# First stage of an attention and mixer kernel: root and evictions in front of scalings, one scaling on VectorE, token products by x tile

## The chip, the cores and the metric

The kernel runs on one core of a Trainium2 chip. A core has five engines with an instruction queue each: TensorE (PE; its weight loads are listed apart as PEld), VectorE (DVE), ScalarE (ACT), GpSimd (POOL) and SyncE (SP, which here only issues transfers). They work side by side and wait for one another through semaphores. The metric is the device time of one execution in microseconds (us); before the change it is 775.88 us, the median of three runs from 775.59 to 776.39.

## The reference

Two blocks in a row, in float32. Attention without a softmax, for each of 8 batches and 8 heads, with a norm over the head's 64 columns:

```
kv  = einsum('bhsd,bhse->bhde', k, v)          # k, v, q: (8, 8, 576, 64)
out = einsum('bhsd,bhde->bhse', q, kv)
rms = sqrt(mean(out * out, axis=-1) + 1e-06)
x   = out / rms * g_norm                       # then (8, 576, 512), heads side by side
```

A mixer over x: first along the sequence (tokens), then along the columns (channels), each with its residual:

```
h  = relu(xt @ w_tok1) @ w_tok2                # xt: x with its last axes swapped
u  = x + h transposed
out = u + relu(u @ w_ch1) @ w_ch2
```

Here w_tok1 is 576 x 256, w_tok2 256 x 576, w_ch1 512 x 1536 and w_ch2 1536 x 512.

## The kernel before, in words

Batches are worked in pairs, four of them. A sequence of 576 rows is cut into four tiles of 128 rows and a rest of 64; the rests of the two batches of a pair share a ninth tile. So a pair has x tiles 0 to 3 (first batch), 4 to 7 (second batch) and 8 (both rests). In the step names a group `c` is two of these tiles: `c` 0 and 1 belong to the first batch, 2 and 3 to the second, 4 is the rest.

The order of the work is written out by hand, as lists of strings: `start` for the attention of the first pair, `middle` for the second pair's attention between the first pair's token mixing, `steady` for the others; the channel part follows. `play` goes through a list and calls each named step, and all engines get their instructions in just this order. An instruction that waits holds up those behind it on the same engine, and no others. The steps around the change are:

- `kv{s}{h}`: k by v of batch `s` of the pair, one half of the heads: 40 instructions on PE, into a PSUM tile ps_kv. `e{s}{h}` evicts it to SBUF as kvp (line 389 on DVE for the first batch of the first pair, else the helper's line 132 on ACT).
- `a{c}{t}`: q by kvp for one x tile, into one of two PSUM buffers, ps_o (ps_r for the rest). All matmuls are recorded at line 135.
- `q{c}{t}`: the squares of that result (ACT, line 455); `g{c}{t}`: the result times g_norm, to x (DVE, line 451). These two read the PSUM buffer, one after the other, and free it.
- `t{c}{t}`: sums of squares (DVE, line 472); `m{c}`: mean (DVE, line 477); `r{c}`: square root (ACT, line 482); `i{c}`: four small DVE instructions (lines 486 to 491) that give the inverse with a correction step.
- the scaling of an x tile by its inverse: `s{c}{t}` on ACT, eight instructions of 64 columns each (line 505), or `d{c}{t}` on DVE, one instruction (line 509).
- `h{s}{t}`: token product for batch `s` and one half `t` of the 256 token columns: the four x tiles of that batch against w_tok1, added up in a PSUM buffer ps_h. `h0{t}{j}` is the part of x tile `j` alone, and exists for the first batch. A float32 matmul is two PE instructions. `hr` adds the rest tile and applies the relu.
- `w{n}{k}`: steps that fetch and decode one block of the token weights: `k` 0 fetches, 1 is two ACT instructions, 2 to 4 are DVE instructions. Blocks 0 and 1 and the rest block 2 hold w_tok1, blocks 3 and 4 hold w_tok2.
- `j14`: 14 products of the identity with itself on PE (28 instructions, ps_j), whose result nobody reads (`keep_warm`, line 1332).
- `l{s}`, `lq{s}`, `lr{s}`: loads of k and v, of q, and of the rest of q for a batch of the next pair, issued on SP.

k, v and q of the first two batches are issued ahead of the list (lines 1275 to 1283).

Of the kernel before, what the change touches and what calls it, by code (L numbers as in the profile page):

```python
# [20 lines left out]
def kernel(  # L21
# [39 lines left out]
    J, JJ, HF = 4, 5, 64  # L61
    LO = P * J
    assert D == 64 and DM == 512 and S == LO + HF and B % 2 == 0
    NC, NF, NTOK = DM // P, DCH // P, DTOK // P
# [49 lines left out]
    def do(f, *a, **kw):  # L114
        return lambda: f(*a, **kw)
# [6 lines left out]
    def dma(o, i, engine=nc.sync):  # L122
        keep(engine.dma_start(o, i))  # L123

    def tensor_add(o, a, b, op=ALU.add, engine=nc.vector):
        keep(engine.tensor_tensor(out=o, in0=a, in1=b, op=op))  # L126

    def relu(o, a):
        keep(nc.scalar.activation(o, a, AF.Relu))  # L129

    def copy(o, a):
        keep(nc.scalar.copy(o, a))  # L132

    def matmul(*a, **kw):
        keep(nc.tensor.matmul(*a, **kw))  # L135
# [78 lines left out]
    def get_tok1(i):  # L214

        rows = words(moe_w_tok1)[:LO].rearrange("(i j p) n w -> i p j n w", j=2, p=P)
        return block(2 * DTOK, lambda raw: [(raw.rearrange("p (j n) w -> p j n w", j=2), rows[i])], w_tok1[i])

    def get_tok1_rem():
        w = words(moe_w_tok1)[LO:]  # L220
        return block(DTOK, lambda raw: [(raw[:HF], w), (raw[HF:], w)], w_tok1r)
# [37 lines left out]
    def t_sums(b):  # L259

        def step(o, x, y):
            return lambda: tensor_add(b(o), b(x), b(y), ALU.subtract)

        return [step(5, 7, 1), step(6, 3, 5), step(7, 3, 7), step(4, 2, 6)]
# [92 lines left out]
    def x_of(pair, i):  # L357

        return X[pair, i // 2][:, i % 2]
# [176 lines left out]
    def token_mixing(pair, seeds, aside=()):  # L536
        h1, acc = {}, {}

        def tok1(side, t, js=range(J)):
            if js[0] == 0:  # L540
                acc[side, t] = ps["h"].tile([P, DM], F32, name="ps_h", tag="h")
            for j in js:
                matmul(acc[side, t], lhsT=w_tok1[j // 2][:, j % 2, ts(t, P)],
                                 rhs=x_of(pair, side * J + j), start=(j == 0), stop=False)

        def tok1_rem():
            for t in range(NTOK):
                for side in range(2):
                    r = ds(side * HF, HF)
                    matmul(acc[side, t], lhsT=w_tok1r[r, ts(t, P)],  # L550
                                     rhs=x_of(pair, 8)[r], start=False, stop=True)
            for side in range(2):
                h1[side] = hp_.tile([P, NTOK, DM], F32, name="h1", tag="h1")
                for t in range(NTOK):
                    relu(h1[side][:, t], acc[side, t])

        def seed(i):


            acc[i] = ps["h"].tile([P, DM], F32, name="ps_u", tag="h")  # L560
            copy(acc[i], x_of(pair, i))

        def tok2(i):
            if i not in seeds:
                n = "o" if i in aside else "h"
                acc[i] = ps[n].tile([P, DM], F32, name="ps_u", tag=n)
            first = i not in seeds
            if i < 8:
                for t in range(NTOK):
                    matmul(acc[i], lhsT=w_tok2[:, t, ts(i % J, P)], rhs=h1[i // J][:, t],  # L570
                           start=(first and t == 0), stop=(t == NTOK - 1), skip_group_check=True)
            else:
                for t in range(NTOK):
                    for side in range(2):
                        matmul(acc[i][ds(side * HF, HF)], lhsT=w_tok2[:, t, LO:],
                               rhs=h1[side][:, t],
                               start=(first and t == 0), stop=(t == NTOK - 1), skip_group_check=True)
            x = x_of(pair, i)
            if first:
                tensor_add(x, acc[i], x)  # L580
            else:
                copy(x, acc[i])
            if i == 8:
                dma(u_rest[ts(pair, P)], x, nc.gpsimd)
                for side in range(2):
                    dma(out[2 * pair + side, LO:], x[ds(side * HF, HF)], nc.gpsimd)
            elif i % 2 == 1:
                dma(
                    u_rows(2 * pair + i // J)[ds((i % J - 1) * P, 2 * P)]
                    .rearrange("(t p) e -> p t e", p=P), X[pair, i // 2], nc.gpsimd)  # L590

        steps = {f"h{s}{t}": do(tok1, s, t) for s in range(2) for t in range(NTOK)}
        steps |= {f"h0{t}{j}": do(tok1, 0, t, (j,)) for t in range(NTOK) for j in range(J)}
        steps |= {f"z{i}": do(seed, i) for i in seeds}
        return steps | {"hr": tok1_rem} | {f"u{i}": do(tok2, i) for i in range(9)}

# [659 lines left out]
    def play(lines, after={}, **stages):  # L1256

        for name in " ".join(lines).split():  # L1260
            if name.isdigit():
                for _ in range(int(name)):
                    next(stages["rounding"], lambda: None)()
            elif name[0] == "-":
                stages["before"][name[1:]]()
            else:
                next(stages[s][name] for s in ("attention", "mixing", "more")
                     if name in stages.get(s, ()))()


    tok1 = [get_tok1(i) for i in range(J // 2)] + [get_tok1_rem()]
# [15 lines left out]
    for t in zeroed:  # L1287
# [8 lines left out]

    start = [
        "j14 kv00 e00", "kv01 e01 l0", "a00 g00 q00", "a01 g01 q01 t00 t01 m0 w01",
        "a10 w02 r0 i0 w03 d00 w04 d01 q10 w30 w40 lq0", "a11 q11 g10 g11 w11 j14",
        "h000 h010 w12 w13 w14 t10 t11 m1", "h001 h011", "kv10 e10 r1 i1 d10 s11", "kv11 e11 l1", "a20 q20",  # L1300
        "a21 q21 g20 g21 t20 t21 m2", "h002 h012 r2 i2 d20", "a30 q30 g30", "a31 q31 s21 g31 t30", "h003 h013 t31 m3",
        "a40 q40 r3 i3 d30 s31 g40 t40 m4 r4 w21 i4 s40 lr0 lr1"]
    middle = [
        "kv00 e00 w31 w22 w23 w24", "h10 -lq1 w32 w33 w34", "h11 w41 w42 w43 w44", "kv01 e01", "hr l0 z2",
        "a0 q00 g01 q01 g00 t00 t01", "u0 f0", "u1 z4", "u2", "a1 q10 g11 q11 g10",
        "kv10 kv11 e10 e11 t10 t11 m0 r0 lq0", "u3 z6 i0 d00 s01 d11 f1", "u4 l1", "a2 q20 g21 q21 g20",
        "a4 q40 t20 g41 q41 t21 g40 lr0 lr1", "u5 s10 t40 t41 m2 r2 f2 1", "u6 1 i2 p20 p21 x00", "u7 1 1"]
# [13 lines left out]
    attentions += [attention(p, ((0, 1), (2, 4), (3,))) for p in range(1, B // 2)]  # L1321

    mixings = [token_mixing(p, (2, 4, 6)) for p in range(B // 2 - 1)]
    mixings.append(token_mixing(B // 2 - 1, range(2, 9), (0, 1)))
    more = {f"w{n}{k}": f for n, b in enumerate(tok1 + tok2) for k, f in enumerate(b)}
    more |= {f"f{n}": b[0] for n, b in enumerate(channel)}
# [5 lines left out]
    def keep_warm(n):  # L1332

        o = ps["h"].tile([P, DM], F32, name="ps_j", tag="h")
        for _ in range(n):
            matmul(o[:, :P], lhsT=ident, rhs=ident, start=True, stop=True)

    more |= {f"j{n}": do(keep_warm, n) for n in (14,)}
    play(start, attention=attentions[0], mixing=mixings[0], more=more)
    play(middle, attention=attentions[1], mixing=mixings[0], before=attentions[0],  # L1340
         more=more, rounding=rounding)
    for n in range(1, B // 2 - 1):
        play(steady[n - 1], attention=attentions[n + 1], mixing=mixings[n], before=attentions[n] | {"u8": mixings[n - 1]["u8"]},
             more=more, rounding=rounding)
# [16 lines left out]
    more = {f"c{i}": f for i, f in enumerate(t_sums(lambda n: uT[0][:, SB[n]]))}  # L1361
# [98 lines left out]
```

## Time and profile before

One execution was profiled. Its own time is 776.08 us; its span, from the first to the last instruction, is 774.3 us.

| what | us |
|---|---|
| median of three runs | 775.88 |
| profiled execution | 776.08 |
| its span | 774.3 |
| PE busy | 762.2 (98%) |
| DVE busy | 641.8 (83%) |
| ACT busy | 279.2 (36%) |
| POOL busy | 112.2 (14%) |
| mean granted TensorE clock | 0.998 |

The page of a profile names lines of the kernel as L135. It gives the busy time of each engine, the chain of work that ended last (followed back from the last instruction, at each step to what released it), and the busy time in stretches of the span. A busy PE is not PE at its peak: matmuls overlap, and their ends are modelled. In the first 120 us the 16 DMA engines are busy nearly all the time and move 351 GB/s in the mean; over the whole span it is 243 GB/s. Idle time of an engine that doesn't set the end costs nothing.

### The profile page before, as it was taken

The numbers are of one execution on the slowest core, as the hardware profiler recorded it, in microseconds if no ns is written. First come the engines' busy times: TensorE is split into PE (matmuls) and PEld (weight loads), VectorE is DVE, ScalarE is ACT, GpSimd is POOL, SyncE is SP. The second block draws the span as 40 slices with busy tenths as digits, with TensorE's granted clock in tenths as the row PEclk, the third lists the DMA queues.
The fourth block names the chain that finished last, engine by engine and source line by source line (L and its number), as shares of the span: only waits on it lengthen the run. The fifth ranks groups of instructions, "written<-read, shape, count | busy, mean of one in ns | idle before, by whom it ended". The sixth has DMA issues, their size and how long they took to land.

```text
span 774.3 us, 12686 instructions
## 1 busy us (share of the span) xinstructions
PE 762.2 (98%) x4690; PEld 614.2 (79%) x4690; DVE 641.8 (83%) x944; ACT 279.2 (36%) x563; POOL 112.2 (14%) x124
## 2 busy tenths in 40 slices
PE   6899999999999999999999999999999999999998
PEld 6656554544888888888888888888888888888887
DVE  2667888797776868989978889996998997798996
ACT  2376574766110133522133252223352223325221
POOL 1002111113410000002240000142000218000204
PEclk9999999999999999999999999999999999999999
DMA  8999999399699796598898578999659879955689
GB/s 313 329 338 375 384 369 347 129 285 356 240 289 344 265 300 196 152 292 174 239 220 268 160 193 247 238 202 260 202 155 284 173 217 206 205 156 149 150 204 119
DMA packets 137819, 188.29 MB, mean 243 GB/s; under 512 B 48800, under 2 KB 95392, under 8 KB 135712
## 3 DMA queue, kind: packets, MB, share of 16 engines
q1 hardware_dynamic: 101744, 167.54, 69.4%
q0 software_dynamic: 34816, 18.36, 16.1%
q10 hardware_dynamic: 1200, 1.61, 0.6%
q8 instruction: 37, 0.61, 0.3%
q14 instruction: 22, 0.18, 0.1%
HBM read 138.31 MB, written 49.15 MB: 242 GB/s over the span
## 4 chain that ended last, share of the span: by engine, by line
PE 97%; DMA 2%; ACT 0%; DVE 0%; SPq 0%; issue 0%
PE ps_d L135 28%; PE ps_b L135 19%; PE ps_a L135 19%; PE ps_h L135 8%; PE ps_u L135 8%; PE ps_v L135 5%; PE ps_c L135 3%; PE ps_o L135 3%; PE ps_kv L135 2%; PE ps_w L135 2%; DMA qT<-in_q_dram 2%; PE ps_j L135 0%; PE ps_r L135 0%; ACT x L505 0%; SPq L123 0%; DVE x L451 0%
## 5 line engine op out<-in xcount | busy, mean ns | idle before, releaser
L135 PE MATMUL ps_d<-ui,w 128*128 128x256 f32 x504 | 118.6, 379 | 0.0
L135 PEld LDWEIGHTS ps_d<-ui,w 128*128 128x128 f32 x504 | 95.8, 190 | 13.0
L132 ACT COPY ps_d<-ps_a 128x768 f32<-128x768 f32 (+1 forms) x56 | 32.0, 572 | 200.5 <-PE ps_a L135 197.5
L126 DVE TENSOR_TENSOR v<-v,v 128x1536 f32<-128x1536 f32 (+2 forms) x70 | 103.2, 1482 | 0.3
L135 PE MATMUL ps_b<-sv,w 128*128 128x256 f32 x324 | 78.9, 380 | 0.0
L135 PE MATMUL ps_a<-v,w 128*128 128x256 f32 x324 | 78.8, 379 | 0.0
L1205 POOL DMA_DIRECT2D out_dram<-us x24 | 26.7, 1833 | 291.8 <-ACT p L132 286.5
L135 PEld LDWEIGHTS ps_b<-sv,w 128*128 128x128 f32 x324 | 61.2, 190 | 8.9 <-issue 0.6
L135 PEld LDWEIGHTS ps_a<-v,w 128*128 128x128 f32 x324 | 61.6, 190 | 8.3
L135 PE MATMUL ps_u<-h,w_tok 128*128 128x512 f32 (+1 forms) x160 | 64.7, 599 | 0.0
L135 PE MATMUL ps_d<-v,w 128*128 128x256 f32 x258 | 62.7, 379 | 0.0
L129 ACT ACTIVATE v<-v 128x768 f32<-128x768 f32 (+1 forms) x54 | 42.6, 821 | 55.1 <-DVE v L126 50.6
L135 PE MATMUL ps_h<-x,w_tok 128*128 128x512 f32 x128 | 58.4, 607 | 0.0
L1205 POOL DMA_DIRECT2D out_dram<-r x40 | 41.3, 1928 | 102.0 <-ACT p L132 80.3
L135 PE MATMUL ps_d<-sv,w 128*128 128x256 f32 x228 | 55.4, 379 | 0.0
L135 PEld LDWEIGHTS ps_d<-v,w 128*128 128x128 f32 x258 | 49.0, 190 | 6.6
L135 PEld LDWEIGHTS ps_u<-h,w_tok 128*128 128x128 f32 (+1 forms) x160 | 25.6, 179 | 31.1 <-issue 26.7
L135 PEld LDWEIGHTS ps_d<-sv,w 128*128 128x128 f32 x228 | 43.3, 190 | 5.9
L135 PE MATMUL ps_a<-uT,w 128*128 128x256 f32 x192 | 46.7, 379 | 0.0
L135 PEld LDWEIGHTS ps_h<-x,w_tok 128*128 128x128 f32 x128 | 24.1, 194 | 28.3 <-issue 25.3
L135 PE MATMUL ps_b<-ui,w 128*128 128x256 f32 x168 | 40.8, 379 | 0.0
L135 PEld LDWEIGHTS ps_a<-uT,w 128*128 128x128 f32 x192 | 36.5, 190 | 4.9
(165 smaller groups left out, 1293.0 us busy)
## 6 DMA issues: line engine op xcount, KB each, us to landing
w<-parts SPq DMA_DIRECT2D x168, 384.0 KB, 3.8
w<-parts SPq DMA_DIRECT2D x56, 192.0 KB, 3.8
uT<-blocks SPq DMA_DIRECT2D x36, 256.0 KB, 5.8
k_in<-in_k_dram SPq DMA_DIRECT2D x8, 1024.0 KB, 11.8
qT<-in_q_dram SPq DMA_DIRECT2D x8, 1024.0 KB, 11.0
out_dram<-x POOLq DMA_DIRECT2D x16, 512.0 KB, 7.2
v_in<-in_v_dram SPq DMA_DIRECT2D x7, 1024.0 KB, 14.4
raw<-in_moe_w_ch_dram SPq DMA_DIRECT2D x8, 768.0 KB, 9.3
```

The lines of the kernel that those rows point to most:

```text
L126: keep(engine.tensor_tensor(out=o, in0=a, in1=b, op=op))
L129: keep(nc.scalar.activation(o, a, AF.Relu))
L132: keep(nc.scalar.copy(o, a))
L135: keep(nc.tensor.matmul(*a, **kw))
L1205: keep(nc.gpsimd.dma_start(to, t()[ds(b * Q, Q), at].rearrange("p n l j -> p n (l j)"), accum_op=ALU.add))
```

## The change

In `start`, `r1` (the root for the first batch's second group) moves from behind `kv10 e10` to the end of the line of `m1`, ahead of `h001 h011`. `i1` and `d10`, which followed it, move behind `kv11 e11`, so that both evictions `e10` and `e11` come ahead of them in the list. The ACT scaling `s11` is replaced by the DVE scaling `d11`. The second filler, between the first pair's second group of attention and its first token products, has 10 products in place of 14.

In `middle`, the token products of the second batch, `h10` and `h11`, are split by x tile: the products with its first two x tiles (`h100 h110 h101 h111`) come first of all, ahead of `kv00`, and those with its other two tiles (`h102 h112 h103 h113`) behind it. The decoding steps keep their places relative to one another; `w31` and `w22` to `w24` are now ahead of `kv00 e00`. `-lq1` (the load of q for batch 3, named so because it belongs to the first pair's list) comes right behind `kv00 e00`; it is still the first load of `middle`, and no load changes its place among the loads.

```diff
-        steps |= {f"h0{t}{j}": do(tok1, 0, t, (j,)) for t in range(NTOK) for j in range(J)}
+        steps |= {f"h{s}{t}{j}": do(tok1, s, t, (j,)) for s in range(2) for t in range(NTOK) for j in range(J)}
...
-        "a10 w02 r0 i0 w03 d00 w04 d01 q10 w30 w40 lq0", "a11 q11 g10 g11 w11 j14",
-        "h000 h010 w12 w13 w14 t10 t11 m1", "h001 h011", "kv10 e10 r1 i1 d10 s11", "kv11 e11 l1", "a20 q20",
+        "a10 w02 r0 i0 w03 d00 w04 d01 q10 w30 w40 lq0", "a11 q11 g10 g11 w11 j10",
+        "h000 h010 w12 w13 w14 t10 t11 m1 r1", "h001 h011", "kv10 e10", "kv11 e11 i1 d10 d11 l1", "a20 q20",
         "a21 q21 g20 g21 t20 t21 m2", "h002 h012 r2 i2 d20", "a30 q30 g30", "a31 q31 s21 g31 t30", "h003 h013 t31 m3",
         "a40 q40 r3 i3 d30 s31 g40 t40 m4 r4 w21 i4 s40 lr0 lr1"]
     middle = [
-        "kv00 e00 w31 w22 w23 w24", "h10 -lq1 w32 w33 w34", "h11 w41 w42 w43 w44", "kv01 e01", "hr l0 z2",
+        "h100 h110 h101 h111 w31 w22 w23 w24", "kv00 e00 -lq1 w32 w33 w34",
+        "h102 h112 h103 h113 w41 w42 w43 w44", "kv01 e01", "hr l0 z2",
...
-    more |= {f"j{n}": do(keep_warm, n) for n in (14,)}
+    more |= {f"j{n}": do(keep_warm, n) for n in (10, 14)}
```

## The prediction

> **What bounds the kernel now.** I read the page first, then three views of the microseconds around the change: the chain that ended last, the waits of TensorE, and the busy time by stretch. The page's chain is by engine:
>
> ```profile
> PE 97%; DMA 2%; ACT 0%; DVE 0%; SPq 0%; issue 0%
> ```
>
> So nearly every microsecond belongs to TensorE (PE). Next, the two largest waits that the waits view lists for PE from 20 us to the end (it names no others there; columns: total us, times, longest):
>
> ```profile
> PE ps_o L135 <- ACT kvp L132: 1.4, 1, 1.4
> PE ps_o L135 <- DMA qT<-in_q_dram: 0.7, 1, 0.7
> ```
>
> Both are in `a20`, the first product of q with batch 1's k by v. After it PE never stops again, so what PE saves near 30 us reaches the end unless a new wait appears. The chain in order of time (start, us, what) shows who holds `a20`:
>
> ```profile
> 24.76 1.34 PE ps_kv L135 x40
> ...
> 26.12 0.37 ACT kvp L132
> 26.49 0.12 ACT root L482
> ...
> 27.64 2.02 ACT x L505 x8
> 29.65 0.26 ACT kvp L132
> ...
> 29.96 2.23 PE ps_o L135 x12
> 32.19 2.77 PE ps_h L135 x4
> 34.95 1.78 PE ps_o L135 x16
> 36.74 1.72 PE ps_h L135 x4
> ```
>
> The second eviction, `e11` (kvp, second row of that kind), was ready when `kv11` ended, at 24.69 + 2.55 = 27.24 us by PE's timeline, but the eight scalings `s11` (x L505 x8) sit ahead of it on ScalarE (ACT). The last lines show a second loss: four token products take 2.77 us, and four of the same kind take 1.72 us a little later. The stretches tell why (the first clock figure is PEclk, the granted TensorE clock):
>
> ```profile
> 27.35:30.76 3.41, 1.48 (x11) 1.32 (x12) 0.95 (x2) 2.27 (x9) 0.00 (x0) 1.00 1.08 332
> 30.76:34.17 3.41, 3.41 (x11) 2.23 (x10) 1.95 (x4) 1.19 (x2) 0.00 (x0) 0.50 0.96 314
> 34.17:37.59 3.41, 3.41 (x21) 2.51 (x20) 2.96 (x10) 1.56 (x5) 0.00 (x0) 1.00 0.99 341
> 13.69:17.11 3.41, 2.89 (x24) 2.70 (x25) 2.06 (x4) 1.31 (x3) 0.00 (x0) 1.00 1.06 413
> ```
>
> PE was busy for 1.48 of 3.41 us (43%) and then got half the clock for 3.41 us. A stretch with 2.89 of 3.41 (85%) was not punished.
>
> [...]
>
> **The change part by part.**
>
> (1) `r1` goes ahead of `e10`, `kv10` and `h001 h011`. On ACT it only passes `e10` (0.37 us). Its input `m1` ends at 25.31 + 0.17 = 25.48 us, and ACT has idled since 20.3. So `r1` runs at about 25.5 instead of 26.39, and `e10` still starts at 26.12. `i1` on VectorE (DVE; four instructions, 26.64 to 27.60 now) starts about 0.9 us earlier; DVE was waiting for that root (1.15 us idle). It issues no DMA.
>
> (2) `s11` (2.02 us of ACT) goes; `d11`, one DVE instruction of 0.69 us (row of `d10`: 0.69), comes behind `d10`, at about 27.4 to 28.1. Work that hides it: none is needed, DVE has 3.07 us idle there, ahead of `g20`. Were that idle time gone it would delay `g20` by 0.69.
>
> (3) `e11` follows `kv11`: 27.27 to 27.62 in place of 29.56 to 29.91. `a20` itself can't start earlier: q of batch 1 was issued at 13.48 and took 14.3 us to land, 27.8, and nothing in the change touches that transfer. So `a20` starts at 27.91 as now, and doesn't stop after four instructions.
>
> (4) `j10` for `j14`: eight instructions of 0.112 us (28 take 3.13 in the chain) are 0.9 us less filler, of which `h000` can use only what its weights allow: `w04` ends at 20.00 + 0.69 = 20.69, `h000` starts at 21.16 now. 0.4 us of gain, and then `kv10` waits for v of batch 1 (issued at 10.25 and 10.65, its second part 14.0 us to landing, so 24.65; `kv10` starts at 24.69 now). Worth zero, with the transfer as what takes it back. If v came early it would still end at q's landing.
>
> Now PE. Sixteen instructions of `a20 a21` at 0.112, the first 0.07 longer as at 27.91: 1.86 us, to 29.77. `h002 h012`: four at 0.43, 1.72, to 31.49. Now `a30` starts at 34.79: **3.30 us earlier**. The parts: 1.53 of wait (28.43 to 29.96), 2.02 - 1.34 = 0.68 for twelve `ps_o` instructions, 2.81 - 1.72 = 1.09 for the four `ps_h`, both by the half clock but for 0.1 of restart. The half clock goes because the stretch from 27.35 then has only 0.56 us idle (84% busy).
>
> What is late next is DVE. `q20` can start 0.09 us after `a20` ends: 29.13 (30.77 now). `q21` moves from 32.28 to 30.02, 2.26 earlier, and `g21 t20 t21 m2 r2 i2 d20 g30` hang on it. `g30` ends at 36.88 + 0.69 - 2.26 = 35.31. `a40` needs the PSUM buffer that `q30` and `g30` read (ps_o has two). PE gets there at 31.49 + 1.79 + 1.79 = 35.07. A new wait of **0.29 us**, unless `g30` comes sooner.
>
> (5) `h100 h110 h101 h111` come ahead of `kv00`, the other four behind it. Same instructions, no DMA, no new weights. Now PE waits 0.13 us (43.26 to 43.39) for `s31`; that goes: `s31` ends at about 40.6 and `h103` comes at 43. `s21` ends at about 36.3 (ACT: `q31` to 34.25, then 2.02), and `h101` comes at 38.0; `d20` ends at 34.7 for `h100` at 36.3. Two more changes between matmuls of different shape, 0.05 to 0.1 each as at 47.35 to 47.88: 0.15. `e00` moves behind `w31` on ACT (1.36 us): done at about 45.5, needed by `a0` at 48. On SP nothing changes its order: `lq1` was the first load of `middle` and still is, and `l0` behind `kv01` comes with PE. k and v of batch 2 land by 37.1 (issued at 27.79, 9.3 us to landing), `kv00` comes at 40. DVE's `w22 w23 w24` go with `w31`, and `hr` needs them: at 42 against 46.
>
> Sum at `hr`: 3.30 - 0.29 + 0.13 - 0.15 = **2.99 us** (49.19 to 46.20). Later transfers have room: the tightest is q of batch 2, issued at 29.63, 12.8 to landing, 42.4, needed at 51.2 now. The loads behind it follow PE's own progress. So the profiled execution's 776.08 (span 774.3 and 1.8 around it) becomes **773.1** (span 771.3). The median shown, 775.88, is 0.20 below the profiled one; I leave that inside the range.
>
> Bounds for the unknowns. [...] if a run of before isn't caught by a half-clock window, its own waits for `g30` (0.29) and for `s31` (about 0.4 instead of 0.13) show, and it is about 1.1 us shorter; then the gain is 1.9. I take the caught case, since the only execution I can see is that. `g30`'s wait lies between 0 and 0.7 (one DVE instruction late). The filler: 0 to 0.4 gained.
>
> **The rivals.** A tie is within 0.2%, 1.55 us, about what a measurement of this kernel can tell from no change.
>
> A, as summed: 773.1. Its own range is 772.4 (no wait for `g30`, no shape cost, 0.2 for the median) to 773.7.
>
> B, the wait goes but the half clock is not in most runs of before[...]: gain 1.9, 774.0, with 773.7 to 774.5. For it: [...] three runs spread over 0.8 us, about the size of 1.1. Against: the profiled run has it and is only 0.20 above the median.
>
> C, another wait takes the place of the one removed: q's transfer. `a20` now starts 0.14 us after it landed. The DMA share is 1.06 to 1.18 there, all 16 engines full, so a landing 1.5 us later in an ordinary run gives back 1.5 of the 3.0: 774.6 to 775.9. Before, a delay of up to 1.5 would have been hidden behind `e11`. Against: it lands in a steady stream of loads that the change leaves alone.
>
> D, slower: the clock. With less filler PE idles 0.4 us before `h000`, 0.4 before `kv10`, 0.67 before `a20`. The trace shows that 85% busy is enough and 43% isn't; in between I know nothing, and windows here would have 75 to 88%. Each window lost costs up to 3.41 / 2 = 1.7 us. One leaves a gain of 1.3, two give 3.4 for 3.0, and it decides from the second; with three, 773.1 + 5.1 = 778.2. Against: the stretch from 10.3 to 13.7 has 2.16 of 3.40 (64%) by the same view and the clock stayed at 1.00 in the next[...].
>
> **How the numbers follow.** A 0.55, B 0.25, C 0.14, D 0.06. Predicted time: A's, 773.1. The range 772.4 to 775.0 holds A and B but for their tails and a third of C; about 0.19 is outside. Faster by over 0.2% (below 774.33): A, most of B and a little of C: 0.80. Within: the rest, 0.13. Slower: D and a trace of C: 0.07.
>
> **What would show it.** In the changed profile: PE's wait for ACT's kvp gone, that for q of about 0.7 us left; PEclk 1.00 through 27 to 38 us; `h002` at about 29.8, `a30` at 31.5, `hr` at 46.2; a short PE wait at `a40`, put down to DVE x L451; all later stages 3.0 us earlier. Wrong would be: `a20` later than 28.5 (C), 0.50 in a stretch before 35 us (D), or a PE wait after 46 us that isn't there now.

## The result and the profile after

The changed kernel takes 774.12 us, the median of 15 runs from 773.14 to 774.6, against 776.01 for the kernel before in its runs beside it (15, from 775.36 to 777.57). The ratio is 0.9973 with a 95% interval of 0.9965 to 0.9981: 2.1 us, more or less 0.6. The forecast was 773.1, in a range from 772.4 to 775.0. The profiled execution took 774.16 us with a span of 772.3, where 773.1 and 771.3 were forecast.

The waits view of the changed kernel names these waits of PE from 20 us to the end (total us, times, longest):

```profile
PE ps_o L135 <- DMA qT<-in_q_dram: 1.1, 1, 1.1
PE ps_h L135 <- DVE w_tok L188: 0.3, 1, 0.3
PE ps_r L135 <- DVE x L451: 0.2, 1, 0.2
```

The wait for ACT's kvp is gone, and the two small ones are those that the forecast worked out: `h000` behind the decoding of its weights, and `a40` behind `g30`. The wait for q, 0.7 us before, has grown to 1.1. The timeline of ACT (start, duration, and in brackets the idle time before it and who ended it) has both evictions right behind their matmuls, with no scaling between:

```profile
25.73 0.22 ACT L482 ACTIVATE root<-ms 128x16 f32<-128x16 f32 x1 [5.19 <-DVE ms L477]
26.23 0.37 ACT L132 COPY kvp<-ps_kv 128x256 f32<-128x256 f32 x1 [0.29 <-PE ps_kv L135]
27.40 0.37 ACT L132 COPY kvp<-ps_kv 128x256 f32<-128x256 f32 x1 [0.79 <-PE ps_kv L135]
```

And this is PE from `h000` to `hr`, in the timeline of the changed kernel:

```profile
20.95 3.70 PE L135 MATMUL ps_h<-x,w_tok 128*128 128x512 f32 x8 [0.32 <-DVE w_tok L188]
24.61 2.76 PE L135 MATMUL ps_kv<-v_in,k_in 128*64 128x64 f32 x80
28.47 2.02 PE L135 MATMUL ps_o<-kvp,qT 128*128 128x128 f32 x16 [1.10 <-DMA qT<-in_q_dram]
30.33 1.88 PE L135 MATMUL ps_h<-x,w_tok 128*128 128x512 f32 x4
32.05 1.95 PE L135 MATMUL ps_o<-kvp,qT 128*128 128x128 f32 x16
33.83 1.88 PE L135 MATMUL ps_h<-x,w_tok 128*128 128x512 f32 x4
35.93 1.09 PE L135 MATMUL ps_r<-kvp,qR 128*64 128x128 f32 x16 [0.22 <-DVE x L451]
...
46.84 1.99 PE L135 MATMUL ps_h<-x,w_tok1r 64*128 64x512 f32 x8
```

In the profile before, the first group of token products behind `a21`, and `hr`, are these lines:

```profile
31.98 2.98 PE L135 MATMUL ps_h<-x,w_tok 128*128 128x512 f32 x4
...
49.19 1.99 PE L135 MATMUL ps_h<-x,w_tok1r 64*128 64x512 f32 x8
```

`h002`, at 31.98, stood in PE's queue behind the rest of `a20`, which waited for the eviction until 29.96; its x tile had been scaled by 28.33 (`d10`, 27.64 + 0.69).

The sixteen PE instructions of `a20 a21` run in one piece. `h002 h012`, two token products of two instructions each, take 1.88 us instead of 2.98; the pair after them took 1.88 before, too. (Where the prediction says four token products, it counts PE instructions.) The clock in the stretches that answer to those of before:

```profile
27.40:30.80 3.40, 2.33 (x18) 2.12 (x19) 1.34 (x3) 1.18 (x3) 0.00 (x0) 1.00 1.03 334
30.80:34.20 3.40, 3.40 (x21) 2.51 (x20) 2.81 (x8) 1.20 (x4) 0.00 (x0) 1.00 1.01 315
```

`hr` starts at 46.84, where it started at 49.19: 2.35 us earlier. From 67 us to the end the PE instructions of the two profiles run in step, 1.94 us apart. So what happens in the first 67 us is all of it; 0.4 us of the 2.35 get lost between 47 and 67 us (the last section).

Two things need an explanation: why 1.9 to 2.1 us and not 3.0, and which part of the change they come from. The theory was the prediction's: the eviction behind the scalings, and the half clock that its wait brings on, are the whole gain, and q's landing bounds `a20` from then on. The rivals were that the half clock is rare, and that the token products split by x tile carry part of the gain.

### The profile page after: what moved, and what is told of

Its sections match the earlier page's. It is cut to its first block, busy times and chain, and to the rows that moved or that the text cites. A ratio compares the mean times of both kernels' runs of the same rounds, so it can differ in the third digit from the quotient of the medians.

```text
span 772.3 us, 12663 instructions
## 1 busy us (share of the span) xinstructions
PE 761.5 (99%) x4682; PEld 613.5 (79%) x4682; DVE 642.8 (83%) x945; ACT 277.5 (36%) x555; POOL 112.1 (15%) x124
## 4 chain that ended last, share of the span: by engine, by line
PE 95%; DMA 3%; DVE 1%; SPq 0%; ACT 0%; issue 0%; ACTq 0%
PE ps_d L135 28%; PE ps_b L135 19%; PE ps_a L135 19%; PE ps_u L135 8%; PE ps_h L135 7%; PE ps_v L135 5%; DMA qT<-in_q_dram 3%; PE ps_c L135 3%; PE ps_w L135 2%; PE ps_o L135 2%; PE ps_kv L135 2%; PE ps_r L135 0%; DVE x L451 0%; DVE ms L472 0%; SPq L123 0%
```

## The experiments

**The order alone.** The kernel before, with the root and the evictions ahead and `d11` for `s11`; the filler stays at 14 and the products unsplit.

```diff
-        "h000 h010 w12 w13 w14 t10 t11 m1", "h001 h011", "kv10 e10 r1 i1 d10 s11", "kv11 e11 l1", "a20 q20",
+        "h000 h010 w12 w13 w14 t10 t11 m1 r1", "h001 h011", "kv10 e10", "kv11 e11 i1 d10 d11 l1", "a20 q20",
```

> The kernel before with the root and both evictions ahead and d11 for s11, but 14 filler products and the token products of the second batch unsplit. Theory 1 (the eviction behind the scalings and the half clock that its wait brings are the whole gain): at least 1.6 us of the changed kernel's 2.1 us (ratio about 0.9976); in its profile a20 runs in one piece behind q's landing, full clock from 27 to 38 us, and at most 0.4 us of wait for s31 in the unsplit products. Theory 2 (the products split by x tile carry much of it): under 1.0 us, with a wait for ACT x L505 of over 0.8 us near 41 us.

774.58 us, ratio 0.9984 (0.9977 to 0.999): 1.2 us faster, between the two theories. All 21 runs list a clock of 0.999 or 1.000, so the order alone removes the half clock. Its timeline of PE shows why:

```profile
28.35 2.02 PE L135 MATMUL ps_o<-kvp,qT 128*128 128x128 f32 x16 [0.47 <-ACT kvp L132]
...
37.44 1.54 PE L135 MATMUL ps_kv<-v_in,k_in 128*64 128x64 f32 x40 [0.54 <-DMA v_in<-in_v_dram]
38.91 7.13 PE L135 MATMUL ps_h<-x,w_tok 128*128 128x512 f32 x16
```

The bracket names ACT's kvp, the second eviction, which ended at 28.30; q had landed at about 28.2 (issued at 14.1, 14.1 us to landing). The two bounds lie within 0.1 us of each other in this profile, and it doesn't tell which held `a20`. There is no wait for `s31` worth naming (the sixteen products take 7.13 us in one piece), so theory 2's reason falls. But `kv00` of the next pair waits for v of batch 2, 0.54 us ahead of it and about 0.15 within it (1.54 us against 1.39 for `kv01`). The order brings PE to `kv00` before its data. Nobody had expected this.

**The split alone.** The kernel before with the products of the second batch by x tile, and nothing else.

```diff
...
-        "kv00 e00 w31 w22 w23 w24", "h10 -lq1 w32 w33 w34", "h11 w41 w42 w43 w44", "kv01 e01", "hr l0 z2",
+        "h100 h110 h101 h111 w31 w22 w23 w24", "kv00 e00 -lq1 w32 w33 w34",
+        "h102 h112 h103 h113 w41 w42 w43 w44", "kv01 e01", "hr l0 z2",
```

> The kernel before with only the token products of the second batch split by x tile and moved. Theory 1: nothing that can be measured, between 0.2 us faster and 0.2 us slower, as a wait of 0.13 us goes and two more changes of shape cost about as much. Theory 2: 0.5 us or more faster.

775.54 us, ratio 0.9997 (0.9988 to 1.0005): nothing that can be measured, as theory 1 said.

**Filler inside the wait.** The kernel before, with ten short instructions where PE waits for the second eviction.

```diff
             for hp in range(HP):
+                if (c, t, hp) == (2, 0, 2):
+                    for _ in range(5):
+                        matmul(o[:, ts(3, P)], lhsT=ident, rhs=ident, start=True, stop=True)
                 matmul(o[:, ts(hp, P)], lhsT=qT[2 * pair + side][:, hp, ts(2 * (c % 2) + t, P)],
```

> The kernel before with five products of the identity (ten PE instructions, about 1.1 us) inside a20, in the wait for the second eviction, written to a part of ps_o that the real product overwrites. The wait stays, only the clock is to be kept up. If most ordinary runs of the kernel before fall to half clock there as the profiled one did: 0.7 to 1.3 us faster (ratio 0.9983 to 0.9991), and 1.00 in the stretch 30.8 to 34.2. If the half clock is rare in ordinary runs: under 0.4 us. If the fillers themselves push a20: slower by up to 0.2.

775.76 us, ratio 0.9999 (0.999 to 1.0007): a miss by the ratio. The reason is in the spans and clocks that every run lists. The runs of the kernel before are of two sorts. Beside the experiments there were 103 of them: 47 with a mean clock of 0.997 or 0.998 and a median span of 774.7 us (774.4 to 775.2), and 56 with a clock of 0.999 or 1.000 and 773.6 us (773.2 to 774.1). The profiled run of before is of the first sort (0.998), and its PEclk is 0.50 from 30.76 to 34.17 us and 1.00 in the stretches around. By the mean clocks I take such a half clock of 3.41 us to come in 47 of the 103 runs (46%); it costs 774.7 - 773.6 = 1.1 us. Runs of 0.999 or 1.000 are called undisturbed from here on. With the filler all 13 runs are undisturbed, their median span 773.9. The rest of `a20` starts no earlier (30.04, in the profile before 29.96) and the half clock is gone, so in this kernel it is PE's idleness in that wait that brings the half clock on. But 0.3 us are lost against the undisturbed runs of before. PE in that kernel's profile:

```profile
28.41 0.68 PE L135 MATMUL ps_o<-kvp,qT 128*128 128x128 f32 x4 [1.12 <-DVE x L512]
28.93 1.28 PE L135 MATMUL ps_o<-ident 128*128 128x128 f32 x10
30.04 1.57 PE L135 MATMUL ps_o<-kvp,qT 128*128 128x128 f32 x12
```

`a20` starts at 28.41 here, not at 27.91. The bracket names `d10`, which isn't what `a20` reads; q had landed at about 28.2 (issued at 13.5, 14.7 us to landing). The fillers hold the rest of `a20` to 30.04, where the eviction ended at 29.96. That is under 0.1 us, and this execution's own span is 773.6, so it doesn't show where the other runs lose 0.3. If q lands still later, the fillers end later too; that is likely, but no profile shows it.

**q in two halves.** The changed kernel, with q of batch 1 loaded in two transfers, so that `a20` and `a21` need the first alone.

```diff
-            dma(qT[b], q[b].rearrange("(c p) s -> p c s", p=P)[..., :LO])
+            for part in ((slice(0, 2 * P), slice(2 * P, LO)) if b == 1 else (slice(0, LO),)):
+                dma(qT[b][..., part], q[b].rearrange("(c p) s -> p c s", p=P)[..., part])
```

> The changed kernel with q of batch 1 loaded in two halves of the sequence, so that a20 and a21 wait for 512 KB less. If the landing of q is what bounds the changed kernel there: the first half lands about 1.5 us earlier, a20 starts right behind kv11 at about 27.5, PE's wait for q falls from 1.1 to about 0.2 us, and the time is 0.7 to 1.0 us below the changed kernel, 773.2. If DVE's g30 or the smaller packets bind instead: within 0.3 us of the changed kernel, and a longer wait for DVE x L451 at ps_r.

773.33 us, ratio to the kernel before 0.997 (0.9959 to 0.9981). The median span is 770.85 against 772.2 for the changed kernel; the time around the span is 2.25 instead of 1.82 us, for which I know no cause, so 0.8 of the 1.35 us arrive in the time. The timeline:

```profile
27.47 2.15 PE L135 MATMUL ps_o<-kvp,qT 128*128 128x128 f32 x16
29.45 1.88 PE L135 MATMUL ps_h<-x,w_tok 128*128 128x512 f32 x4
```

PE no longer waits for q, and `a20` starts right behind `kv11`, at 27.47 where it was 28.47, as forecast. So q's landing is what bounds the changed kernel here.

**The same halves without the change.** Is q's landing a bound before, too?

> The kernel before with q of batch 1 in two halves and nothing else. If the second eviction behind the scalings sets the end of a20 there, the earlier q is worth nothing: within 0.3 us of the kernel before, its span in runs without a half clock within 0.2 us of 773.6, and the wait for ACT kvp grows by what the wait for q loses. If q was the bound before too: 0.7 us faster.

776.68 us, ratio 1.0005 (0.9997 to 1.0013); span 773.6 in its five undisturbed runs, 774.6 in the eight with a clock of 0.998. Nothing is gained. PE's timeline in the profile, whose mean clock is 0.998, with the half clock from 31.07 on (the four token product instructions at 32.39 take 2.93 us, in the changed kernel 1.88):

```profile
27.52 0.71 PE L135 MATMUL ps_o<-kvp,qT 128*128 128x128 f32 x4
30.32 2.28 PE L135 MATMUL ps_o<-kvp,qT 128*128 128x128 f32 x12 [2.08 <-ACT kvp L132]
```

`a20` starts as early as in the experiment before it, and then waits 2.08 us for the eviction instead of 1.4. The two bounds lie one behind the other: the eviction first, q's landing second.

**Order and halves, products unsplit.** Both of the first and the fourth experiment, without the split and the shorter filler.

> The order and d11 alone, as in the first experiment, with q of batch 1 in two halves; the token products stay unsplit, so that kv00 comes right behind the first pair's last product of q. If the landing of v of batch 2 (37.3 to 38.0 us) bounds kv00 there: a20 starts about 0.8 us earlier and kv00 doesn't, its wait grows from 0.5 to about 1.4 us, and the time is that of the first experiment, 774.6, within 0.3. If that wait was chance: 773.7.

774.85 us, ratio 0.9989 (0.9982 to 0.9995): the first experiment's 774.58 within 0.3. Four of its 21 runs list a clock of 0.997 or 0.998, with spans from 774.2 to 775.0, while the first experiment had none in 21; the median of the other 17 is 774.81. The lines of its timeline:

```profile
27.39 2.15 PE L135 MATMUL ps_o<-kvp,qT 128*128 128x128 f32 x16
...
37.66 1.61 PE L135 MATMUL ps_kv<-v_in,k_in 128*64 128x64 f32 x40 [1.59 <-DMA v_in<-in_v_dram]
```

`a20` is 1.0 us earlier than in the first experiment (28.35), `kv00` isn't (37.66 and 37.44); the wait for v takes all of it. So without the split any gain ahead of `kv00` ends there, and that is what the split is good for: it puts four token products (eight PE instructions, 3.7 us) ahead of `kv00` while v lands. The kernel of the experiment with q in two halves differs from this one by the split and by the shorter filler, which is worth nothing (below): 0.997 (0.9959 to 0.9981) there, 0.9989 (0.9982 to 0.9995) here, two intervals that don't overlap, each against the runs of the kernel before beside it. That a 1.59 us wait for v costs these four runs the clock is a guess: none of them was profiled, and the profiled run has that wait and lists 0.999.

**The scaling left on ScalarE.** The changed kernel with `s11`, now behind `e11`.

```diff
-        ... "kv11 e11 i1 d10 d11 l1", ...
+        ... "kv11 e11 i1 d10 s11 l1", ...
```

> The changed kernel with the eight scalings s11 on ScalarE, behind e11, in place of d11 on VectorE. If the place of the eviction is what counts and the engine of the scaling doesn't: within 0.3 us of the changed kernel (774.1), with q20 about 0.2 us later behind s11. If the scaling has to leave ScalarE: 0.8 us or more slower than the changed kernel.

774.19 us, ratio 0.9974 (0.9968 to 0.9981), as the changed kernel. Its ACT timeline has the eviction ahead of the scalings:

```profile
27.46 0.37 ACT L132 COPY kvp<-ps_kv 128x256 f32<-128x256 f32 x1 [0.79 <-PE ps_kv L135]
27.73 2.02 ACT L505 ACTIVATE x<-x,inv 128x64 f32<-128x64 f32 x8
```

It is the place of the eviction; the engine of the scaling doesn't matter here. `q20` wasn't later behind `s11`, against the forecast: it starts 1.23 us after `a20`, in the changed kernel 1.22.

**The filler.** The changed kernel with 14 products of filler, and with none.

> The changed kernel with 14 products of filler as before. The prediction's worth of the shorter filler is zero, because the landing of v and of q takes it back: within 0.2 us of the changed kernel's 774.1, with a shorter wait for q. If the shorter filler carries some of the gain: 0.4 us slower.

> The changed kernel without its second filler: PE idles for about 2.7 us ahead of h000. The rival of the prediction that feared for the clock: half clock in a window that starts between 19 and 25 us in many runs, the token products take up to 1.7 us longer, of which the waits for v (25.1) and for q (28.3) hide about 1: 0.2 to 0.9 us slower than the changed kernel in the mean, and a mean clock of 0.998 in the runs that it hits. If the filler is not needed: within 0.2 us and no half clock.

With 14: 774.06 us, ratio 0.9974 (0.9963 to 0.9985): the shorter filler is worth nothing. The wait for q isn't shorter, as was expected, but 1.2 us, because q landed later in this profile:

```profile
28.79 2.02 PE L135 MATMUL ps_o<-kvp,qT 128*128 128x128 f32 x16 [1.22 <-DMA qT<-in_q_dram]
```

Without: 773.92 us, ratio 0.9971 (0.996 to 0.9982). Five of its seven runs list a clock of 0.998 or less, with a median span of 772.2, and the other two 771.8 and 771.7. So by the mean clock the half clock does come back, as feared, but it costs about 0.45 us here, and the mean is not slower than with filler, where 0.2 to 0.9 us slower was forecast. That the waits for v and q hide the rest is likely but not shown: the profiled execution is one of the two that kept the clock. The filler is not needed for the time.

**Loads in another order.** The changed kernel with q of batches 0 and 1 in halves, the second block of w_tok1 fetched behind the first half of batch 1's q, and its decoding moved behind `d11`. Of the edit, the lines on the loads and the `w11` taken out of the line above are left out here.

```diff
...
-        "h000 h010 w12 w13 w14 t10 t11 m1 r1", "h001 h011", "kv10 e10", "kv11 e11 i1 d10 d11 l1", "a20 q20",
+        "h000 h010 t10 t11 m1 r1", "h001 h011", "kv10 e10", "kv11 e11 w11 i1 d10 d11 w12 w13 w14 l1", "a20 q20",
```

> The changed kernel with q of batches 0 and 1 in halves, and the second block of w_tok1 fetched behind the first half of batch 1's q in place of ahead of batch 1's k; its decoding (w11 to w14) moves behind e11 and d11. If the landing of v and q of batch 1 is the only bound left: kv10 starts about 1.4 us earlier than in the fourth experiment (at about 23.6), and the time is 0.5 to 1.0 us below its 773.3, the decoding of the second block taking some of it at h002. If VectorE is as close a bound there: within 0.3 us of 773.3, with a wait for w_tok at h000 or h002.

773.29 us, ratio 0.9966 (0.9952 to 0.9979): as with the halves alone, 773.33, and the span is longer (771.3 against 770.85).

```profile
28.03 0.43 DVE L184 TENSOR_SCALAR w_tok<-w_tok 128x512 f32<-128x512 f32 x1 [2.04 <-ACT w_tok L169]
29.79 1.98 PE L135 MATMUL ps_h<-x,w_tok 128*128 128x512 f32 x4 [0.91 <-DVE w_tok L193]
```

`kv10` starts at 24.20, 0.8 us earlier than with the halves alone and not 1.4; `a20`, at 26.74, gains 0.7 us, and the token products behind it wait 0.91 for the decoding. DVE stands idle for 2.04 us ahead of its first decoding step, which waits for the one on ACT (27.33), behind `e11` (26.85 to 27.22). So the next bound here is the decoding in its new place, a chain over both engines. VectorE itself isn't full. The simpler kernel with q in halves is the one to keep; by the medians it is 0.8 us below the changed kernel, though the intervals of the two ratios overlap.

## Why the prediction was right, and by how much it was off

The mechanism is the one that the prediction gave. The eviction left the queue behind the scalings, `a20` ran through, the half clock went (all 15 runs of the changed kernel list 0.999 or 1.000), and all of it but the 0.4 us of the last section reached the end, with no new wait over 0.32 us. The direction and the range held. The likeliest time was 1.0 us too low: 774.12 lies outside A's own 772.4 to 773.7. That it falls into B's 773.7 to 774.5 is in part luck. B took the half clock out of the time before; what made the changed kernel slower than 773.1 was another thing. In the profiled execution the missing 1.0 us is 0.56 for q's landing, 0.4 for a stop of PE near 64 us that nobody had priced, and under 0.1 for the rest. Two terms need a closer account.

- Part (3), q's landing, was taken as 27.8 from the one profile, which had an early one: in the seven other profiles with q in one piece, issue and landing time add up to 28.2 to 28.7. In the changed kernel `a20` starts at 28.47 behind q, with `s11` kept at 28.62, with 14 fillers at 28.79; the profile of the split alone, which leaves `a20` as it was, puts it at 28.44. The 0.56 us in the changed kernel are most of the 0.64 by which `hr` came later than forecast (46.84 against 46.20). The term was sized from a run in which it bound nothing: in the kernel before, by the prediction's estimate, q could come 1.5 us later at no cost. This is the mechanism of rival C, at about a third of its price.

- The half clock was put into the likeliest case because the profile had it. It comes in 46% of the runs of before, and so decides what the gain is measured against, not the time of the changed kernel. Its price was right: 1.1 us by the prediction's own bounds, 1.1 between the two sorts of runs. Against undisturbed runs of before the change gains 773.6 - 772.2 = 1.4 us in span, against disturbed ones 774.7 - 772.2 = 2.5. Weighted, 0.54 x 1.4 + 0.46 x 2.5 = 1.9, close to the 1.9 to 2.1 measured. B's 1.9 was meant for undisturbed runs, which gave 1.4.

Point by point for the rest:

- (1) `r1` ran at 25.73 (25.5 forecast), `e10` at 26.23 (26.12). Right. The earlier root wasn't tried alone. By the changed kernel's profile it isn't needed: `d10 d11` end at 28.26, and `h002` starts at 30.33, so they could come the forecast 0.9 us later; that is an estimate.
- (2) `d11` costs nothing, and the experiment with `s11` shows more: it gains nothing either.
- (4) The filler is worth nothing: measured as such, with 14 and with none.
- `g30`: a wait of 0.22 us at `a40` where 0.29 was forecast (its own figures, 35.31 - 35.07, give 0.24). It appears in seven of the eight profiles in which `a20` runs through; and, as the prediction said of runs without the half clock, in the split's profile, with 0.21.
- (5) The split was priced against the kernel before, at +0.13 and -0.15 us, and alone it is indeed worth nothing. (That PE never stops behind `a20`, as the prediction says at its start, leaves out the 0.13 us that it counts here.) What the step missed is its worth once (3) is done. It checked that v of batch 2 (37.1) lands before `kv00` in its new place (40), and did not ask where `kv00` would stand in the old one: at 36.9, ahead of v's landing. The order alone reached 0.9984, the whole change 0.9973; the medians are 0.46 us apart and the intervals overlap, but the wait of 0.54 us is of the size. With q in halves the split's worth stands clear of the noise.
- Rival D, the clock with less filler: the changed kernel never lost it. Without filler it did, in five of seven runs, and was not slower.

## What to carry to other kernels

An eviction that releases the next matmuls belongs ahead of any work in its engine's queue whose result is needed later; look for it where a copy starts well after its last matmul has ended (here 29.56 against 27.24 us, with 2.02 us of scalings ahead of it). When a wait is taken away, price the next bound from more than one run, since the old wait may have covered its spread, and ask of each other part of the change what it is worth after the first part, not before it. A product that is ready can cover a landing (here 3.7 us of them cover a wait of 1.59 us for v): put it ahead of the one whose data are still under way.

## What the runs showed of the hardware that was not expected

Whether PE falls to half clock differs from run to run of the same kernel: by the mean clock it does in 47 of the 103 runs of before (0.997 or 0.998) and doesn't in 56 (0.999 or 1.000). In the profile before, 3.41 us with 43% of work, in which PE waited for 0.7 and 1.4 us, were followed by the half clock; in that of the split, with the same two waits, PE worked for 1.36 of the 3.40 us from 27.40 on (40%) and the clock stayed at 1.00. So the share of work in such a stretch doesn't decide alone, and the prediction's reading that 43% is too little holds for its one profile. What else decides was not shown.

In the changed kernel's profile the rest products of the second pair take 1.05 us, in the profile before 0.65 for the same 32 instructions. First before, then after:

```profile
65.73 0.65 PE L135 MATMUL ps_r<-kvp,qR 64*64 64x64 f32 x32
```

```profile
63.39 1.05 PE L135 MATMUL ps_r<-kvp,qR 64*64 64x64 f32 x32
```

Up to these lines the two profiles are 2.34 us apart, behind them 1.94. PE stops for 0.4 us in the middle of these products, with nothing that the profile names as the cause. The profile of the order with q in halves has such a stop too, of 0.5 us; in three more (q in halves, the scaling on ScalarE, the loads in another order) the same products take 0.71 to 0.79 us, and in the seven others 0.65. It is the 0.4 us lost between 47 and 67 us; what it is stays open. So does the time outside the span of the kernels with q in halves: 2.25, 2.13, 2.12 and 1.99 us in the median, where the kernel before had 1.83, 1.84, 1.98 and 1.98 in its runs beside them.
